# Values in token pairs, one fixed load order and constants on VectorE in a kernel of windowed attention and an MLP

## Chip, cores and metric

The kernel runs on one core of one Trainium2 chip. The metric is device time in microseconds (us); each number is the median of several executions. TensorE (PE in the profile) multiplies matrices, PEld is its weight load, VectorE is DVE, ScalarE is ACT, GpSimd is POOL, SyncE is SP (SPq is its queue, which issues the DMAs).

## The reference, cut to what matters

```python
# q, k, v: (4 batches, 8 heads, 768 tokens, 64); 4 sink tokens, window 128
scores = q @ k.T / 8
keep = is_sink | in_window            # token sees the 4 sinks and the last 128
a = softmax(where(keep, scores, -1e9))
x = (a @ v) as (3072 tokens, 512)
h = x @ w_in                          # 512 x 2048, "up projection"
out = (h * sigmoid(1.702 * h)) @ w_out   # 2048 x 512, "down projection"
```

All inputs and the output are fp32 in HBM; the kernel computes in fp16. It works on 12 tiles of 256 tokens (three per batch).

## The kernel before

All work is recorded as operations with estimated durations. A planner inside the kernel then picks, on each engine, the operation that can start first, and that gives the order of every engine's instruction stream. The order of each stream is then fixed, so a wrong estimate or a late load holds up everything behind it. One queue (SyncE) issues nearly all loads and all stores.

Weights come in eight chunks of 1 MB in fp32 through two staging buffers, and GpSimd casts each in two halves:

```python
def weights(j, at):
    dst = w32[j % RW]                        # RW = 2
    war = reuse("w32", j % RW)               # wait for the casts of chunk j - 2
    ...
    o_l = op("SP", 420, (2700,), lambda: nc.sync.dma_start(dst, src), war, prio=at, kind="w")
    for n in range(2):
        ...
        o = op("POOL", 1170, 1300, lambda to=to, fr=fr: nc.gpsimd.tensor_copy(out=to, in_=fr), [o_l], ...)
```

q and k are loaded with two neighbouring tokens per partition, so a contiguous piece is 2 x 64 x 4 = 512 B. v is loaded so that row p of half i holds token 2p + i, which makes 256 B pieces and four DMAs per tile; one GpSimd cast follows:

```python
for j in range(2):
    for i in range(2):
        def f(i=i, j=j):
            nc.sync.dma_start(
                dv[64 * i : 64 * i + 64, j],
                v[b, :, t0 + P * j : t0 + P * j + P].rearrange("h (p i) d -> i p h d", i=2)[i],
            )
...
def f():
    nc.gpsimd.tensor_copy(out=w16[:, :, :, 0:D], in_=dv)
```

Constants (ones columns, zeroed sink keys `ks16`, zeroed sink values `vs16`) are set by GpSimd; the sink values are loaded in fp32 and cast by GpSimd into `vs16`.

The softmax here doesn't subtract the row's maximum and nothing guards it: scores larger than these inputs give would overflow.

## Time and profile before

| | before |
|---|---|
| time, median | 260.92 us |
| profiled span | 258.1 us |
| time between the start of tile 7's and tile 10's up projection | 55.2 us (18.4 per tile) |
| last chunk of w_out landed | 98.9 us |
| first matmul of tile 7's up projection | 159.6 us |

(A landing is the end of a DMA in the trace. The start of a tile's projection is found by counting: the up projection has 768 matmul records, 64 per tile, in order.)

The page's slices, from kernel before. Each digit is the busy share of one fortieth of the span in tenths; PEclk is the TensorE clock that was granted, GB/s what the DMA moved.

```profile
PE   8987897799959969999999999999999999999991
PEclk9997999999998997999999999999999999999999
DMA  7999999999999999893310110111011011011132
GB/s 208 227 230 343 211 222 216 346 230 207 240 355 226 209 316 254 199 221 84 83 43 0 43 41 3 41 43 24 19 42 44 1 43 41 3 41 43 41 70 51
```

The DMA is full for the first 18 slices (6.45 us each, so to about 116 us). TensorE has gaps in the first 16 (103 us) and is then full to the end. Where the GB/s are over 340, weights are moving; where they are 207 to 230, q, k and v are.

The same in four stretches of the kernel before: busy us (number of instructions) of each engine, then granted clock, DMA share and GB/s.

```profile
core 0: us, PE busy (x) PEld busy (x) DVE busy (x) ACT busy (x) POOL busy (x), PEclk, DMA share, GB/s
0.00:30.00 30.00, 25.20 (x336) 20.20 (x337) 20.73 (x49) 12.21 (x25) 21.30 (x51) 0.94 1.05 241
30.00:60.00 30.00, 26.28 (x324) 20.88 (x322) 25.79 (x63) 19.46 (x40) 19.03 (x29) 1.00 1.17 258
60.00:104.00 44.00, 38.60 (x415) 27.12 (x412) 30.27 (x70) 24.39 (x51) 20.82 (x31) 0.92 1.08 254
104.00:240.00 136.00, 136.00 (x1210) 87.68 (x1209) 72.31 (x160) 69.26 (x130) 12.73 (x24) 1.00 0.23 52
```

From 104 us TensorE is busy 136.00 of 136. What can be gained lies before.

Who uses the staging buffers of the weights, kernel before: durations min/median/max in ns, first and last start, then who waited for these instructions (us, times).

```profile
L303 POOL CAST w_in<-w x8: 1036/1042/1504, 21.3 to 52.5; 128x1024 f16<-128x1024 f32 x8
L303 POOL CAST w_out<-w x8: 1041/1044/1047, 75.7 to 100.0; 128x1024 f16<-128x1024 f32 x8
...
who waited for it (us, times):
  PE bank L580: 5.1, 2
...
  PEld L552: 3.1, 4
  PE bank L552: 2.2, 2
```

DMA packets by size, kernel before. Of those under 512 B, 24,576 are v's (one of 256 B for each of 3072 tokens and 8 heads).

```profile
DMA packets 59074, 34.22 MB, mean 133 GB/s; under 512 B 27048, under 2 KB 52008, under 8 KB 59048
```

### The profile page before, as it was taken

The numbers are of one execution on the slowest core, as the hardware profiler recorded it, in microseconds if no ns is written. First come the engines' busy times: TensorE is split into PE (matmuls) and PEld (weight loads), VectorE is DVE, ScalarE is ACT, GpSimd is POOL, SyncE is SP. The second block draws the span as 40 slices with busy tenths as digits, with TensorE's granted clock in tenths as the row PEclk, the third lists the DMA queues.
The fourth block names the chain that finished last, engine by engine and source line by source line (L and its number), as shares of the span: only waits on it lengthen the run. The fifth ranks groups of instructions, "written<-read, shape, count | busy, mean of one in ns | idle before, by whom it ended". The sixth has DMA issues, their size and how long they took to land.

```text
span 258.1 us, 5883 instructions
## 1 busy us (share of the span) xinstructions
PE 238.5 (92%) x2344; PEld 162.4 (63%) x2344; DVE 151.8 (59%) x345; ACT 129.0 (50%) x250; POOL 73.9 (29%) x133
## 2 busy tenths in 40 slices
PE   8987897799959969999999999999999999999991
PEld 8755675687835854444566667666666666666640
DVE  4866899689952983100167766776766666553310
ACT  0726495468742762211265575555557557533411
POOL 8666657661545248200010130131300000000000
PEclk9997999999998997999999999999999999999999
DMA  7999999999999999893310110111011011011132
GB/s 208 227 230 343 211 222 216 346 230 207 240 355 226 209 316 254 199 221 84 83 43 0 43 41 3 41 43 24 19 42 44 1 43 41 3 41 43 41 70 51
DMA packets 59074, 34.22 MB, mean 133 GB/s; under 512 B 27048, under 2 KB 52008, under 8 KB 59048
## 3 DMA queue, kind: packets, MB, share of 16 engines
q1 hardware_dynamic: 57816, 33.10, 56.3%
q10 hardware_dynamic: 1232, 0.75, 1.0%
q8 instruction: 18, 0.29, 0.5%
q14 instruction: 8, 0.07, 0.2%
HBM read 27.56 MB, written 6.29 MB: 131 GB/s over the span
## 4 chain that ended last, share of the span: by engine, by line
PE 66%; DMA 18%; SPq 6%; POOL 4%; issue 2%; DVE 1%; ACT 0%; ACTq 0%; POOLq 0%
PE bank L580 31%; PE bank L552 23%; DMA w<-in_moe_w_in_dram 6%; DMA qk<-in_q_dram 5%; SPq L349 5%; PE bank L498 3%; PE bank L444 3%; DMA w<-in_moe_w_out_dram 3%; PE bank L407 3%; POOL qk L371 2%; DMA v<-in_v_dram 2%; DMA mask<-cmask 2%; PE bank L523 1%; SPq L339 1%; DMA qk<-in_k_dram 1%
## 5 line engine op out<-in xcount | busy, mean ns | idle before, releaser
L580 PE MATMUL bank<-w_out,gT 128*128 128x512 f16 x384 | 101.8, 387 | 5.1 <-POOL w_out L303 5.1
L552 PE MATMUL bank<-xT,w_in 128*128 128x256 f16 x768 | 102.4, 274 | 2.3 <-POOL w_in L303 2.2
L552 PEld LDWEIGHTS <-w_in 128*128 128x128 f16 x768 | 72.2, 98 | 21.3 <-POOL w_in L303 3.1
L566 DVE SCALAR_TENSOR_TENSOR gT<-th,bank 128x512 f16<-128x512 f16 x96 | 65.1, 679 | 28.9 <-ACT th L564 28.8
L564 ACT ACTIVATE th<-bank 128x512 f16<-128x512 f32 x96 | 57.5, 599 | 46.9 <-PE bank L552 44.7
L459 ACT ACTIVATE at<-bank 128x512 f16<-128x512 f32 (+1 forms) x96 | 48.6, 565 | 22.2 <-PE bank L444 22.2
L580 PEld LDWEIGHTS <-gT 128*128 128x128 f16 x384 | 35.3, 99 | 28.5 <-issue 8.4
L371 POOL CAST qk<-qk 128x512 f16<-128x512 f32 x44 | 27.7, 658 | 55.3 <-PE bank L407 50.2
L465 DVE TENSOR_TENSOR at<-at,mask 128x1024 f16<-128x1024 f16 (+1 forms) x48 | 35.4, 738 | 8.5 <-ACT at L459 8.0
L531 DVE COPY xT<-bank 128x256 f16<-128x256 f16 x48 | 13.7, 285 | 29.4 <-ACT th L564 21.7
L600 ACT ACTIVATE osb<-bank 128x512 f32<-128x512 f32 (+1 forms) x25 | 14.3, 579 | 28.9 <-PE bank L580 28.9
L415 DVE COPY qkT<-bank 128x512 f16<-128x512 f16 x48 | 20.0, 419 | 9.8 <-PE bank L407 9.3
L498 PE MATMUL bank<-v,at 128*128 128x65 f16 x352 | 21.7, 194 | 0.9 <-DVE at L465 0.9
L481 ACT ACTIVATE ats<-bank 128x256 f16<-128x256 f32 x32 | 12.4, 386 | 19.4 <-PE bank L474 14.2
L498 PEld LDWEIGHTS <-at 128*128 128x128 f16 x352 | 17.9, 98 | 5.6 <-DVE at L465 1.6
L515 DVE TENSOR_TENSOR xn<-bank,rcp 128x256 f16<-128x256 f32 x48 | 20.2, 422 | 1.1
L383 POOL CAST v<-v 128x1024 f16<-128x1024 f32 x12 | 13.0, 1080 | 27.0 <-DMA v<-in_v_dram 18.0
L407 PE MATMUL bank<-ident,qk 128*128 128x128 f16 x192 | 18.3, 220 | 0.9 <-POOL qk L371 0.7
L444 PE MATMUL bank<-qkT 64*128 64x256 f16 x192 | 16.2, 246 | 0.8 <-DVE qkT L415 0.4
L513 DVE RECIPROCAL rcp<-bank 128x4 f32<-128x4 f32 x48 | 8.5, 176 | 12.7 <-PE bank L498 9.3
L407 PEld LDWEIGHTS <-qk 128*128 128x128 f16 x192 | 12.2, 97 | 5.8 <-issue 3.5
L498 PE MATMUL bank<-vs,ats 128*128 128x65 f16 x128 | 15.4, 195 | 0.2
(24 smaller groups left out, 121.0 us busy)
## 6 DMA issues: line engine op xcount, KB each, us to landing
v<-in_v_dram SPq DMA_DIRECT2D x48, 128.0 KB, 5.7
out_dram<-osb SPq DMA_DIRECT2D x46, 128.0 KB, 2.4
qk<-in_q_dram SPq DMA_DIRECT2D x11, 512.0 KB, 6.2
qk<-in_k_dram SPq DMA_DIRECT2D x11, 512.0 KB, 8.0
w<-in_moe_w_in_dram SPq DMA_DIRECT2D x4, 1024.0 KB, 7.9
w<-in_moe_w_out_dram SPq DMA_DIRECT2D x4, 1024.0 KB, 7.8
qk<-in_k_dram ACTq DMA_DIRECT2D x4, 128.0 KB, 3.0
qk<-in_q_dram SPq DMA_DIRECT2D x4, 128.0 KB, 3.2
```

The lines of the kernel that those rows point to most:

```text
L371: nc.gpsimd.tensor_copy(out=c16[:, :, e, h].rearrange("s i h d -> s h i d"), in_=dst[:, e, h])
L407: nc.tensor.transpose(ps[:, e, :, i, :], c16[:, i, e, 2 * p : 2 * p + 2].rearrange("s h d -> s (h d)"), ident)
L415: o_cp = op("DVE", 331, 430, lambda: nc.vector.tensor_copy(out=T, in_=f16(o_tp).rearrange("d (e j s) -> d e j s", e=2, j=2)), [o_tp] + war ...
L444: nc.tensor.matmul(f32(o_s, i)[:, c : c + w], src[d, 1, j], T[d, 0].rearrange("d j s -> d (j s)")[:, q0 : q0 + w], start=True, stop=True,)
L459: nc.scalar.activation(out=A[:, i, 0:W], in_=f32(o_s, i)[:, 0:W], func=AF.Exp, scale=scale)
L465: nc.vector.tensor_tensor(out=A[:, :, 0:W], in0=A[:, :, 0:W], in1=mask[:, c0 : c0 + W].unsqueeze(1).to_broadcast((P, 2, W)), op=ALU.mult,)
L498: nc.tensor.matmul(ps[:, j, i], a_, v_, start=(n == 0), stop=(n == len(mms) - 1))
L515: o_n = op("DVE", 300, 425, lambda: nc.vector.tensor_tensor(out=X, in0=avp()[:, :, :, 0:D], in1=rc.to_broadcast((P, 2, 2, D)), op=ALU.mult ...
L552: nc.tensor.matmul(f32(holder[0])[:, bass.ts(e, TB)], w_in16[:, c, bass.ts(Fi, P)], X[:, c], start=(c == 0), stop=(c == NP - 1),)
L564: o_t = op("ACT", 477, 600, lambda first=first: nc.scalar.activation(out=th[first.places[0]], in_=f32(first), func=AF.Tanh, scale=0.851), ...
L566: o_g[k, s] = op("DVE", 565, 690, lambda first=first, s=s: nc.vector.scalar_tensor_tensor(out=g[:, 2 * s : 2 * s + 2].rearrange("p a t -> ...
L580: nc.tensor.matmul(f32(holder[0]), g[:, Fi, bass.ts(j, P)], w_out16[:, Fi], start=(Fi == 0), stop=(Fi == NF - 1),)
```

## The change

Its intent: full-size packets for v, weights early, and a shorter start. v is loaded like q and k; the rows then sit at the wrong partitions, so four casts of 64 partitions put them right. All big loads are chained in one order of priority: tiles 0 and 1, all of w_in, tile 2, all of w_out, then tiles 3 to 11. Weights get a third staging buffer. Constants go to VectorE, and the sink values are cast by a DMA issued by GpSimd. Attention outputs and their transposes may hold two PSUM banks (of the eight in TensorE's result memory) each instead of one.

```diff
-    RS, RQ, RV, RKT, RA, RX, RG, RTH, RO, RW = 3, 2, 4, 9, 6, 3, 5, 3, 3, 2
+    RS, RQ, RV, RKT, RA, RX, RG, RTH, RO, RW = 3, 2, 4, 9, 6, 3, 5, 3, 3, 3
-    plan = Plan(8, {"s": 4, "k": 1, "t": 2, "a": 1, "x": 1, "h": RTH, "o": 2})
+    plan = Plan(8, {"s": 4, "k": 1, "t": 2, "a": 2, "x": 2, "h": RTH, "o": 2})
+    o_ks0 = op("DVE", 600, 700, lambda: nc.vector.memset(ks16, 0.0), ...)
+    def vs_const():
+        nc.vector.memset(vs16, 0.0)
...
+            nc.gpsimd.dma_start(
+                vs16[32 * i : 32 * i + 4, :, :, i, 0:D], v[:, i::2, 0:n_sink, :].rearrange("b h t d -> t b h d")
+            )
...
-        for j in range(2):
-            for i in range(2):
-                ...                                  # four loads of 64 partitions
+        o_lv = op("SP", 450, (1790,), lambda: nc.sync.dma_start(
+            dv, v[b, :, t0 : t0 + TB].rearrange("h (p i) d -> p h i d", i=2)), war, prio=prio + 0.6, kind="load")
...
-            nc.gpsimd.tensor_copy(out=w16[:, :, :, 0:D], in_=dv)
+        for j in range(2):
+            for i in range(2):
+                    nc.gpsimd.tensor_copy(
+                        out=w16[64 * i : 64 * i + 64, j, :, 0:D], in_=dv[64 * j : 64 * j + 64, :, i]
+                    )
...
+    loads.sort(key=lambda o: (o.prio, o.seq))
+    for a_, b_ in zip(loads, loads[1:]):
+        b_.behind = a_                               # the planner starts b_ only after a_
```

(Cut: the planner's test of `behind`, its new estimates for DMA latency, and the order of the small loads: the identity goes from SyncE's queue to ScalarE's, the mask after it.)

More of the change, by code (lines that the diff above doesn't have):

```diff
@@ L44 @@
         "eng", "dur", "lat", "fn", "deps", "prio", "acq", "rel", "start", "end", "left", "users",
-        "seq", "banks", "places", "kind",
+        "seq", "banks", "places", "kind", "behind",
     )
@@ L53, in __init__ @@
         self.users = []
-        self.banks = None
+        self.banks = self.behind = None
 HOP = {
@@ L97, in could @@
         def could(o, t):
+            if o.behind and o.behind.start is None:
+                return None
             s = max([t] + [after(d, o) for d in o.deps])
@@ L140, in run @@
             if isinstance(o.lat, tuple):
-                begin = max(s + 1500, dma_free)
+                begin = max(s + 2000, dma_free)
                 dma_free = begin + o.lat[0]
-                o.end = dma_free + 500
+                o.end = dma_free + 300
             else:
@@ L208 @@
     w32 = ring("w32", RW, (P, 4, 512), FP32)
-    vs32 = pool.tile([P, B, NP, D], FP32, name="vs32")
     vs16 = pool.tile([P, B, NP, 2, E], FP16, name="vs16")
-    ks16 = ring("ks16", B * NP, (P, P), FP16)
+    ks16 = pool.tile([P, B * NP, P], FP16, name="ks16")
     qk32 = ring("qk32", RS, (P, 2, H, 2, D), FP32)
-    v32 = ring("v32", RS, (P, 2, H, D), FP32)
+    v32 = ring("v32", RS, (P, H, 2, D), FP32)
     qk16 = ring("qk16", RQ, (P, 2, 2, H, D), FP16)
@@ L248 @@
     o_zero = op("DVE", 100, 200, lambda: nc.vector.memset(zero, 0.0), prio=NEVER, kind="const")
-    o_ident = op("SP", 420, (140,), lambda: nc.sync.dma_start(ident, ident_d.ap()), prio=NEVER + 2.3, kind="load")
-    o_mask = op("ACT", 420, (400,), lambda: nc.scalar.dma_start(mask, mask_d.ap()), prio=NEVER + 3, kind="load")
-    o_vs0 = op("POOL", 1800, 2000, lambda: nc.gpsimd.memset(vs16, 0.0), prio=NEVER + 120, kind="const")
-    def vs_ones():
+    o_ident = op("ACT", 420, (140,), lambda: nc.scalar.dma_start(ident, ident_d.ap()), prio=NEVER + 2.6, kind="load")
@@ L254, in vs_ones, with ones @@
+    o_mask = op("ACT", 420, (400,), lambda: nc.scalar.dma_start(mask, mask_d.ap()), prio=NEVER + 4, kind="load")
+    def ones():
+        for t in v16:
+            nc.vector.memset(t[:, :, :, D : D + 1], 1.0)
+    o_ones = op("DVE", 250, 350, ones, prio=NEVER + 1, kind="const")
+    o_ks0 = op("DVE", 600, 700, lambda: nc.vector.memset(ks16, 0.0), prio=NEVER + 2, kind="const")
+    def vs_const():
+        nc.vector.memset(vs16, 0.0)
         for i in range(2):
-            nc.gpsimd.memset(vs16[32 * i : 32 * i + 4, :, :, i, D : D + 1], 1.0)
@@ L257 @@
-    o_vs1 = op("POOL", 300, 400, vs_ones, [o_vs0], prio=NEVER + 121, kind="const")
+            nc.vector.memset(vs16[32 * i : 32 * i + 4, :, :, i, D : D + 1], 1.0)
+    o_vs0 = op("DVE", 700, 800, vs_const, prio=NEVER + 3, kind="const")
     def vs_load():
         for i in range(2):
-            nc.sync.dma_start(
-                vs32[32 * i : 32 * i + 4], v[:, i::2, 0:n_sink, :].rearrange("b h t d -> t b h d")
-            )
-    o_vsl = op("SP", 900, (300,), vs_load, prio=NEVER + 10, kind="load")
@@ L267, in vs_cast @@
-    def vs_cast():
-        for i in range(2):
-            r = slice(32 * i, 32 * i + 4)
-            nc.gpsimd.tensor_copy(out=vs16[r, :, :, i, 0:D], in_=vs32[r])
-    o_vsc = op("POOL", 2400, 2500, vs_cast, [o_vsl, o_vs1], prio=NEVER+122, kind="vs")
-    o_ks0 = []
-    for u in range(B * NP):
-        o_ks0.append(
-            op("POOL", 150, 250, lambda u=u: nc.gpsimd.memset(ks16[u], 0.0), prio=NEVER + 12 + 40 * (u // NP), kind="const")
-        )
-    o_one = []
-    for i in range(RV):
-        o_one.append(
-            op("POOL", 120, 220, lambda i=i: nc.gpsimd.memset(v16[i][:, :, :, D : D + 1], 1.0),
-               prio=NEVER + 10 + i, kind="const")
-        )
+            nc.gpsimd.dma_start(
+                vs16[32 * i : 32 * i + 4, :, :, i, 0:D], v[:, i::2, 0:n_sink, :].rearrange("b h t d -> t b h d")
+            )
@@ L287 @@
+    o_vs = op("POOL", 2000, (300,), vs_load, [o_vs0], prio=NEVER + 10, kind="load")
     o_win, o_wout = {}, {}
+    loads = []
     def weights(j, at):
@@ L295, in weights @@
             src = moe_w_out[bass.ts(j - 4, 512), :].rearrange("(c p) f -> p c f", p=P)
-        o_l = op("SP", 420, (2700,), lambda: nc.sync.dma_start(dst, src), war, prio=at, kind="w")
+        o_l = op("SP", 450, (3000,), lambda: nc.sync.dma_start(dst, src), war, prio=at, kind="w")
+        loads.append(o_l)
         for n in range(2):
@@ L334, in f @@
                         )
-                    lq[p, e] = op(eng, 420, (432,), f, war, prio=NEVER + 2.5 + p / 8, kind="load")
+                    lq[p, e] = op(eng, 500, (450,), f, war, prio=NEVER + 2.5 + p / 8, kind="load")
         else:
@@ L341, in f @@
                     )
-                o = op("SP", 420, (1730,), f, war, prio=prio + e, kind="load")
+                o = op("SP", 450, (1790,), f, war, prio=prio + e / 2, kind="load")
+                loads.append(o)
                 for p in range(NP):
                     lq[p, e] = o
-        lv = []
-        for j in range(2):
-            for i in range(2):
-                def f(i=i, j=j):
-                    nc.sync.dma_start(
-                        dv[64 * i : 64 * i + 64, j],
-                        v[b, :, t0 + P * j : t0 + P * j + P].rearrange("h (p i) d -> i p h d", i=2)[i],
-                    )
-                lv.append(op("SP", 420, (560,), f, war, prio=prio + 2 + i, kind="load"))
+        o_lv = op("SP", 450, (1790,), lambda: nc.sync.dma_start(
+            dv, v[b, :, t0 : t0 + TB].rearrange("h (p i) d -> p h i d", i=2)), war, prio=prio + 0.6, kind="load")
+        loads.append(o_lv)
         c16 = qk16[k % RQ]
@@ L380, in load, with f @@
         war = reuse("v16", k % RV)
-        def f():
-            nc.gpsimd.tensor_copy(out=w16[:, :, :, 0:D], in_=dv)
-        o_cv[k] = op("POOL", 1200, 1300, f, lv + war + [o_one[k % RV]],
-                     prio=(nominal(k - 1, -4) if k else NEVER + 5), kind="cv")
-        uses("s32", sl, o_cv[k])
+        o_cv[k] = []
+        for j in range(2):
+            for i in range(2):
+                def f(j=j, i=i):
+                    nc.gpsimd.tensor_copy(
+                        out=w16[64 * i : 64 * i + 64, j, :, 0:D], in_=dv[64 * j : 64 * j + 64, :, i]
+                    )
+                o = op("POOL", 560, 660, f, [o_lv] + war + [o_ones],
+                       prio=(nominal(k - 1, -4) if k else NEVER + 5), kind="cv")
+                o_cv[k].append(o)
+                uses("s32", sl, o)
     k_ap = k
@@ L423, in ks @@
                     nc.gpsimd.tensor_copy(
-                        out=ks16[NP * b + p][d, 32 * i : 32 * i + 4].rearrange("d (a i) -> d i a", i=2),
+                        out=ks16[d, NP * b + p, 32 * i : 32 * i + 4].rearrange("d (a i) -> d i a", i=2),
                         in_=T[d, 1, 0].rearrange("d (i a) -> d i a", i=2)[:, :, 0:2],
                     )
-            o_ks[b, p] = op("POOL", 260, 400, ks, [o_cp, o_ks0[NP * b + p]], prio=base - 4 * h8, kind="ks")
+            o_ks[b, p] = op("POOL", 260, 400, ks, [o_cp, o_ks0], prio=base - 4 * h8, kind="ks")
             uses("qkT", u % RKT, o_ks[b, p])
@@ L474, in sk @@
                 nc.tensor.matmul(
-                    f32(o_k)[:, 0:TB], ks16[NP * b + p], T[:, 0].rearrange("d j s -> d (j s)"),
+                    f32(o_k)[:, 0:TB], ks16[:, NP * b + p], T[:, 0].rearrange("d j s -> d (j s)"),
                     start=True, stop=True,
@@ L500, in attention @@
         dur = 12 * 31 if r else 6 * 31
-        deps = [o_m, o_cv[k]] + ([o_se, o_cv[k - 1], o_vsc] if r else [])
+        deps = [o_m, *o_cv[k]] + ([o_se, *o_cv[k - 1], o_vs] if r else [])
         o_a = op("PE", dur, dur + 166, av, deps, prio=base - 1.5 * h8, acq=("a", 1), kind="av")
```

## The prediction

> What bounds the kernel now. The median is 260.94 us, the profiled span 258.1. The slices show two stages. Up to about 115 us the DMA is full (9 tenths in nearly every slice) and TensorE has gaps; from 104 us TensorE runs back to back (20.00 us busy in each 20 us window) until its last matmul at 252.4, a tail of 5.7. In steady state a tile of 256 tokens costs 18.4 us (up projection of tile 7 starts at 159.6, of tile 10 at 214.8), all TensorE. The chain of waits agrees: DMA 18%, queue issue 6%, nearly all before 100 us. So the loss is TensorE's starved time before 104 us.
>
> What changes.
> - v packets. 24,832 packets of 256 B (27.9 ns mean, 43.3 us over 16 engines) beside 24,576 of 512 B for q and k (32.9 ns). v now gets half as many of 512 B, as q, about 25 us: 18 us less. The records add up to 1.1 times the elapsed time there, so about 1.3 us per tile, 16 in all. The Trainium skill, "DMA: Bandwidth & Descriptors", Specifications, gives 512 B as the minimum for line rate; this trace agrees: 9.2 B/ns against 15.6 per engine. v takes 12 issues instead of 48.
> - Load order. w_in goes straight after tile 1, w_out after tile 2, with three staging buffers. Before, the last w_out landed at 98.9 us, and the first down projection waited for it while tiles 3 to 8 were loaded. This is the larger part: the dense stretch can start after three tiles.
> - GpSimd casts v in four pieces of 64 partitions, about 0.6 us each instead of one of 1.08: plus 1.2 us per tile. It loses memsets (5 us) and the 2.4 us sink cast.
> - Constants on VectorE fall where it idles until q arrives (0.9 to 3.1 us): nothing. The casting DMA is needed only at 18 us: nothing.
>
> Estimate. Rates from landings: 1 MB of weights 2.9 us, 512 KB of q, k or v 1.95. Tile 0's q and k are in at 8.2 as now, v at 9.4, tile 1 at 15.3, w_in at 26.9, tile 2 at 32.8, w_out at 44.4; two casts of 1.05 make it usable at 46.5. The new instruction order puts half of the first down projection and two pieces of the up projection after that (about 5 us), so the steady pattern starts with tile 2's up projection at 52. Five tiles at 18.4 lead to tile 7's at 144, where it was at 159.6; from there the TensorE order is the same, 92.8 us to the last matmul and 5.7 to the end. Span 242.5, time about 245. The gain, 16 us, is TensorE idle time before 52.
>
> Expected: 244.5 us, range 238 to 251; faster by over 2% 0.94, within 2% 0.05, slower 0.01.
>
> Shown right by: the last w_out landing near 44 instead of 99 us; no 256 B packets but the sinks'; TensorE's dense stretch beginning near 50; the tile period unchanged at 18.4; loads done near 100 instead of 115.
>
> What would make it wrong: GpSimd (about 32 us of casts before 46) falling behind the weights, since VectorE's mask multiply and GpSimd slow each other (that multiply took 0.55 to 1.10 us here); output stores queued behind blocked loads on the single queue; a lower TensorE clock in the denser start (0.83 in three windows before); or the w_in reload waiting for its buffer.

## More of the kernel before

The casts of w_out are spread from 75.7 to 100.0 us, and the down projection (L580) waited 5.1 us for them, in two waits of 2.8 and 2.3 us. The up projection (L552) waited for w_in.

## The result and the profile after

| | before | after |
|---|---|---|
| time, median | 260.92 us | 246.81 us |
| ratio to before, 95% interval | | 0.9466 [0.9429, 0.9504] |
| profiled span | 258.1 us | 244.4 us |
| last chunk of w_out landed | 98.9 us | 46.0 us |
| start of tile 7's up projection | 159.6 us | 146.4 us |
| tile 7 to tile 10 | 55.2 us | 55.1 us |

A ratio is the mean time of one kernel's fast runs over that of the other's of the same rounds, so it is not quite the ratio of the medians quoted. In the kernel after, source lines have moved: the up projection is L544 (was L552), the down projection L572 (L580), weight casts L294 (L303), q and k casts L357 (L371), v casts L373 (L383).

The page's slices, kernel after:

```profile
PE   8968899999999999999999999999999999999991
PEclk9999999999999999999999999999999999999998
DMA  6999999999999914902901101101101101101132
GB/s 175 263 340 329 334 355 347 305 288 302 247 293 303 290 58 112 236 3 58 285 4 43 46 3 43 42 4 46 43 3 46 43 3 43 44 2 46 43 73 55
```

The stretches of the kernel after (columns as before):

```profile
0.00:30.00 30.00, 24.16 (x333) 19.26 (x334) 23.40 (x61) 12.22 (x25) 20.50 (x34) 1.00 0.99 288
30.00:60.00 30.00, 29.82 (x308) 21.14 (x306) 20.38 (x47) 17.15 (x35) 23.73 (x37) 1.00 1.09 318
60.00:104.00 44.00, 44.00 (x457) 29.93 (x454) 30.17 (x68) 26.29 (x52) 21.49 (x35) 1.00 0.85 223
```

Weight casts and who waited for them, kernel after:

```profile
L294 POOL CAST w_in<-w x8: 1037/1164/1499, 19.6 to 29.4; 128x1024 f16<-128x1024 f32 x8
L294 POOL CAST w_out<-w x8: 1035/1165/1498, 36.8 to 47.0; 128x1024 f16<-128x1024 f32 x8
...
who waited for it (us, times):
  POOL w_out L294: 2.3, 3
  POOL w_in L294: 1.3, 3
```

And its packets:

```profile
DMA packets 46618, 34.20 MB, mean 140 GB/s; under 512 B 2304, under 2 KB 39552, under 8 KB 46592
```

What to see: TensorE is full after the first 5 slices (30 us) instead of 16. It was busy 29.82 of 30 us between 30 and 60, and 44.00 of 44 between 60 and 104. Nobody on TensorE waits for a weight cast any more; the only one listed is GpSimd itself, waiting for its next chunk. v's small packets are gone. The first 30 us did not improve: 24.16 us busy against 25.20, and those figures include filler matmuls that are meant to keep the clock up.

Then a surprise: TensorE's total busy time fell from 238.5 to 233.1 us, though the matmuls are the same but for the fillers (136 and 131). The clock explains most of that. Three windows of the kernel before, each 3.41 us long, which the trace records at half clock:

```profile
21.61:25.02 3.41, 2.65 (x23) 2.15 (x24) 1.54 (x3) 1.87 (x4) 2.53 (x3) 0.50 1.12 324
76.22:79.63 3.41, 2.79 (x7) 1.01 (x7) 0.00 (x0) 0.00 (x0) 2.82 (x4) 0.50 1.17 310
96.70:100.11 3.41, 2.99 (x12) 1.11 (x12) 0.29 (x1) 0.44 (x2) 2.48 (x4) 0.50 1.16 318
```

And the 3.41 us just before each of them:

```profile
18.20:21.61 3.41, 2.26 (x34) 1.26 (x31) 3.12 (x6) 3.25 (x9) 1.38 (x2) 1.00 1.06 384
72.81:76.22 3.41, 1.22 (x12) 0.95 (x10) 2.03 (x4) 1.41 (x4) 1.69 (x2) 1.00 1.05 385
93.29:96.70 3.41, 1.53 (x21) 1.09 (x20) 2.88 (x7) 1.88 (x4) 1.45 (x2) 1.00 1.03 378
```

TensorE was busy for only 2.26, 1.22 and 1.53 us of these, and was then run at half clock for one window. In the second and third it waited for w_out (2.8 and 2.3 us, the waits above); in the first mainly for VectorE's mask multiplies and copies. In the three slow windows it was busy 8.43 us at half clock, so about 4.2 us of its work would have fitted into half the time: an estimate of 4.2 us lost, of the 5.4 us difference in busy time. The profiled run of the kernel after has no such window before its last matmul. The Trainium skill, "TensorE: Matmul & The Clock Gate", Part 1, describes this gate as half rate after an idle window of about 3.4 us; the length agrees with the 3.41 us here, but the windows that led to it were a third to two thirds busy.

### The profile page after: what moved, and what is told of

Same layout as the page of the kernel before. It is cut to its first block, busy times and chain, and to the rows that moved or that the text cites. A ratio compares the mean times of both kernels' runs of the same rounds, so it can differ in the third digit from the quotient of the medians.

```text
span 244.4 us, 5826 instructions
## 1 busy us (share of the span) xinstructions
PE 233.1 (95%) x2339; PEld 160.0 (65%) x2339; DVE 154.7 (63%) x353; ACT 129.4 (53%) x250; POOL 87.3 (36%) x146
## 2 busy tenths in 40 slices
DMA packets 46618, 34.20 MB, mean 140 GB/s; under 512 B 2304, under 2 KB 39552, under 8 KB 46592
## 4 chain that ended last, share of the span: by engine, by line
PE 84%; DVE 6%; DMA 4%; ACT 2%; issue 0%; ACTq 0%; DVEq 0%
PE bank L572 34%; PE bank L544 33%; PE bank L490 5%; PE bank L436 5%; PE bank L399 5%; DVE at L457 3%; DMA mask<-cmask 3%; PE bank L515 2%; DVE xn L507 1%; PE bank L466 1%; ACT at L451 1%; DMA ident<-cident 1%; DVE gT L558 1%; ACT th L556 0%; ACT ats L473 0%; DVE xT L523 0%
## 5 line engine op out<-in xcount | busy, mean ns | idle before, releaser
L572 PE MATMUL bank<-w_out,gT 128*128 128x512 f16 x384 | 107.0, 379 | 0.0
L544 PE MATMUL bank<-xT,w_in 128*128 128x256 f16 x768 | 103.0, 273 | 0.7 <-DVE xT L523 0.6
L544 PEld LDWEIGHTS <-w_in 128*128 128x128 f16 x768 | 72.7, 98 | 22.9 <-issue 2.4
L572 PEld LDWEIGHTS <-gT 128*128 128x128 f16 x384 | 33.4, 98 | 9.9 <-issue 0.2
L357 POOL CAST qk<-qk 128x512 f16<-128x512 f32 x44 | 26.9, 643 | 34.1 <-PE bank L399 31.6
L373 POOL CAST v<-v 64x512 f16<-64x512 f32 x48 | 31.2, 649 | 14.7 <-PE bank L490 11.8
L399 PE MATMUL bank<-ident,qk 128*128 128x128 f16 x192 | 18.4, 221 | 0.4 <-DVE qk L348 0.2
L415 POOL COPY ks<-qkT 64x4 f16<-64x4 f16 x32 | 8.9, 277 | 26.2 <-DVE qkT L407 22.6
L515 PEld LDWEIGHTS <-xn 128*128 128x128 f16 x96 | 8.7, 98 | 11.6 <-DVE xn L507 2.8
```

Of the source, the lines that this page charges most:

```text
L357: nc.gpsimd.tensor_copy(out=c16[:, :, e, h].rearrange("s i h d -> s h i d"), in_=dst[:, e, h])
L373: nc.gpsimd.tensor_copy(out=w16[64 * i : 64 * i + 64, j, :, 0:D], in_=dv[64 * j : 64 * j + 64, :, i])
L399: nc.tensor.transpose(ps[:, e, :, i, :], c16[:, i, e, 2 * p : 2 * p + 2].rearrange("s h d -> s (h d)"), ident)
L544: nc.tensor.matmul(f32(holder[0])[:, bass.ts(e, TB)], w_in16[:, c, bass.ts(Fi, P)], X[:, c], start=(c == 0), stop=(c == NP - 1),)
L572: nc.tensor.matmul(f32(holder[0]), g[:, Fi, bass.ts(j, P)], w_out16[:, Fi], start=(Fi == 0), stop=(Fi == NF - 1),)
```

## The experiments

Twelve kernels ran. Names A to E are the theories, as the expectations introduce them. Ratios are to the kernel before in the same rounds; its median was 262.08, 260.98 and 261.12 us in the three groups.

| run | median us | ratio | 95% interval |
|---|---|---|---|
| e1_v256 | 248.65 | 0.9497 | [0.9464, 0.9531] |
| e2_pairs_only | 251.50 | 0.9595 | [0.9563, 0.9627] |
| e9_order_only | 250.01 | 0.9545 | [0.9520, 0.9571] |
| e3_free_order | 249.48 | 0.9539 | [0.9487, 0.9592] |
| after_again (control) | 246.92 | 0.9460 | [0.9426, 0.9494] |
| e5_rw4 | 247.96 | 0.9501 | [0.9467, 0.9535] |
| e6_mask | 246.04 | 0.9436 | [0.9397, 0.9475] |
| e13_vs_pool | 246.87 | 0.9463 | [0.9430, 0.9496] |
| e7_consts | 249.43 | 0.9559 | [0.9521, 0.9596] |
| e8_banks1 | 248.18 | 0.9521 | [0.9483, 0.9560] |
| e15_v0_act | 244.86 | 0.9396 | [0.9353, 0.9439] |
| e16_v0_act_mask | 244.87 | 0.9395 | [0.9353, 0.9436] |

All were correct. The planner makes a new TensorE order for most of these edits (in e1_v256, e5_rw4, e13_vs_pool and the control it is that of the changed kernel, fillers aside), so a run compares two plans, not one load alone. Not tested alone: the third staging buffer, the planner's new DMA estimates, and the identity's move to ScalarE's queue.

### Packets or order?

**The changed kernel with v in 256 B packets.** The instruction order of TensorE is the same.

```diff
-    o_lv = op("SP", 450, (1790,), lambda: nc.sync.dma_start(dv, v[...].rearrange("h (p i) d -> p h i d", i=2)), ...)
+    def f_lv():                       # the four loads of the kernel before, in one planned operation
+        for j in range(2):
+            for i in range(2):
+                nc.sync.dma_start(dv[64 * i : 64 * i + 64, j], v[...].rearrange("h (p i) d -> i p h d", i=2)[i])
-    in_=dv[64 * j : 64 * j + 64, :, i]
+    in_=dv[64 * i : 64 * i + 64, j]
```

> The changed kernel with v loaded as before, in four issues of 256 B packets per tile; casts stay in four pieces (no rows moved), and the instruction order on every engine stays that of the changed kernel. Theory A (the load order is the larger part, and TensorE has some slack): the last w_out lands about 4 us later (three v tiles at 1.35 us), near 50 us, and the time is 248 to 251 us. Theory B (the packets are the larger part): 254 us or more.

It took 248.65 us: 1.8 us over the changed kernel by the medians, but 0.8 us by the ratios (this group's kernel before was slower too), with overlapping intervals. The last w_out landed at 49.5 us instead of 46.0, but tile 2's up projection started at 53.8 instead of 52.6. So 3.5 us of later loading cost 1.2 us: with weights early, the packets hardly matter. Theory B falls for this kernel; the time and the landing are those of Theory A. One down projection did wait here, 1.1 us, for a cast of w_out; in the changed kernel none did.

**The kernel before with token pairs alone.**

```diff
-    four loads "h (p i) d -> i p h d" and one cast of 128 partitions
+    one load "h (p i) d -> p h i d" and four casts of 64 partitions (as in the change)
```

> The kernel before with v loaded in token pairs (512 B packets, one issue per tile) and cast in four pieces, nothing else; two staging buffers for weights and the load order are left to its planner. Theory A (order is the larger part): the last w_out still lands after 85 us and the time stays at 254 us or more. Theory B (packets): 250 us or less. Theory C (the two overlap, since either lets TensorE fill the same idle time): this and e9_order_only each give more than 8 of the 14 us.

251.50 us: 10.6 us of gain by this part alone, far more than A allowed. The last w_out landed at 84.3 us instead of 98.9, in the old order. Who waited for weight casts in this run:

```profile
who waited for it (us, times):
  PEld L549: 1.1, 1
  PE bank L549: 0.8, 1
```

The down projection's waits of 5.1 us are gone (only the up projection, here L549, waits), and with them both half-clock windows near 76 and 97 us; this trace has 6.8 us at half clock, all near 16 to 22 us.

**The kernel before with the fixed order and the third buffer alone.**

```diff
+    "behind", and loads.sort(...); b_.behind = a_     (as in the change)
-    RW = 2
+    RW = 3
```

> The kernel before with the one fixed load order and three staging buffers for weights, nothing else: v still comes in 256 B packets, constants and casts stay on GpSimd. Theory A: 248 to 251 us, as e1_v256. Theory B: 255 us or more. Theory C: about 250 us, and e2_pairs_only close to it.

250.01 us: 12.1 us of gain, with v still in 256 B packets. Together with the run above this is Theory C: one part alone gives 4.05%, the other 4.55%, both with the rest of the change 5.34%, not 8.6%. Both fill the same idle time of TensorE. Once it is full, more loading speed buys little. The run e7_consts below supports this: it has fixed order, third buffer, token pairs and second banks together, with the constants on GpSimd as here, and is no faster (0.9559) than this run without token pairs and second banks (0.9545).

**The changed kernel without the chain that fixes the order.**

```diff
-    for a_, b_ in zip(loads, loads[1:]):
-        b_.behind = a_
```

> The changed kernel without the chain that fixes the load order: its planner then puts the fourth w_in and all of w_out after more tiles (a staging buffer that is not free lets other loads pass). Theory A: slower than the changed kernel by 3 us or more (250 or over), with the last w_out landing after 50 us. Theory B: within 1.5 us of the changed kernel's 246.8.

249.48 us. The planner put the last two chunks of w_out after tile 7, and the last landed at 73.7 us. The interval just overlaps the changed kernel's, so a cost of 2.7 us by the medians, 1.9 by the ratios, is likely, not certain, and lies between what Theories A and B allowed (its profiled run, the slowest of its four, also has a half-clock window from 10.71 to 14.12 us). It is small beside the 28 us by which w_out is later, because TensorE then has up projections and attention of other tiles to do.

### What sets the place of the dense stretch?

The dense stretch is the part in which TensorE has no gaps. The prediction took the last landing of w_out (Theory D). The view of the weight casts in the profile after says otherwise: no matmul waited for w_out. Theory E is that TensorE is dense from 29 us on and that the start-up of the first two tiles decides.

**The control.** 

> The changed kernel itself, as the control for the three runs beside it: ratio to the kernel before 0.945 to 0.950 by every theory.

246.92 us, 0.9460: the first result repeats. Its trace, too, has no half-clock window before the last matmul.

**A fourth staging buffer.** `RW = 4` instead of 3, the same TensorE order.

> The changed kernel with four staging buffers for weights instead of three; the TensorE order stays the same. The fourth w_in and the fourth w_out no longer wait for a cast, so the last w_out lands 1.5 to 2.5 us earlier. Theory D (the prediction's: TensorE's dense stretch is set by the last w_out's landing): 1.5 to 2.5 us faster than the control. Theory E (TensorE has been dense since about 29 us, and its position is set by the start-up of the first two tiles' attention): within 0.5 us of the control.

247.96 us, not faster. But the premise failed: the last w_out landed at 45.4 us, against 45.2 in the control. Probably the wait for a buffer had been hidden behind other transfers. So this run does not tell D from E; it shows only that the fourth buffer brings nothing.

**The mask early.** 

```diff
-    o_mask = op("ACT", 420, (400,), lambda: nc.scalar.dma_start(mask, ...), prio=NEVER + 4, ...)
+    o_mask = op("SP", 420, (400,), lambda: nc.sync.dma_start(mask, ...), prio=NEVER + 2.95, ...)
```

> The changed kernel with the mask's load issued on the SyncE queue before tile 0's v and tile 1, so that it lands near 8 us instead of 11.7. VectorE waited 1.5 us for it before the first mask multiply. Theory E: 0.7 to 1.5 us faster than the control. Theory D: within 0.5 us.

246.04 us; 0.9 us under the control by the medians, but the intervals overlap widely, so nothing is shown by the time. The trace shows why little came of it. VectorE in the changed kernel's first profile, in the control's, then in this run (start us, length us, what, and in brackets the idle time before it and what ended it):

```profile
11.78 3.30 DVE L457 TENSOR_TENSOR at<-at,mask 128x768 f16<-128x768 f16 x4 [1.54 <-DMA mask<-cmask]
15.01 0.17 DVE L505 RECIPROCAL rcp<-bank 128x4 f32<-128x4 f32 x1
```

```profile
10.65 2.37 DVE L457 TENSOR_TENSOR at<-at,mask 128x768 f16<-128x768 f16 x4
15.15 0.18 DVE L505 RECIPROCAL rcp<-bank 128x4 f32<-128x4 f32 x1 [2.13 <-PE bank L490]
```

```profile
9.34 0.56 DVE L457 TENSOR_TENSOR at<-at,mask 128x768 f16<-128x768 f16 x1 [0.33 <-ACT at L451]
...
12.42 0.56 DVE L457 TENSOR_TENSOR at<-at,mask 128x768 f16<-128x768 f16 x1 [0.87 <-ACT at L451]
15.11 0.18 DVE L505 RECIPROCAL rcp<-bank 128x4 f32<-128x4 f32 x1 [2.13 <-PE bank L490]
```

Against the first profile the multiplies start 2.4 us earlier and the last ends at 13.0 instead of 15.1, but the next instruction starts at 15.11, not earlier than 15.01: it waits 2.13 us for the attention output, and that needs v, which landed at 10.8 us and which GpSimd was still casting. The wait moved. In the control, the same kernel as the first profile, the mask had landed in time (10.0 us) without the edit, and VectorE waited the same 2.13 us; so the mask was not the limit. This run's profile also has one half-clock window (22.93 to 26.34 us) that the control lacks. A multiply took 0.55 to 0.56 us here; in the first profile, beside GpSimd's v casts, the four took 0.65, 0.96, 0.96 and 0.96. The Trainium skill, "SBUF — State Buffer", Who interferes with whom, says that a VectorE instruction with two SBUF inputs contends with a GpSimd instruction that reads SBUF; these numbers agree.

**Sink constants on GpSimd.** 

```diff
-    nc.vector.memset(vs16, 0.0)  and two small ones
+    nc.gpsimd.memset(vs16, 0.0)  and two small ones, op("POOL", 2300, 2400, ...)
```

> The changed kernel with the sink values' constants (one memset of 128x2080, 1.79 us on VectorE, and two small ones) set on GpSimd, which is idle there, instead of VectorE. The first q cast on VectorE can start near 3.5 us instead of 4.83. If those constants delay the start-up (against the prediction's 'nothing'): 0.5 to 1.2 us faster than the control. If the last k piece's landing (9.1 us) and the mask's set the end of tile 0's attention anyway: within 0.4 us.

246.87 us, as the control. VectorE's first q cast started at 3.64 instead of 4.83 us, and nothing came of it. The prediction had these constants end by 3.1 us; they ended at 4.8, and it did not matter.

**Constants and sinks all on GpSimd, as before.**

```diff
-    memsets on VectorE; sinks by a casting DMA into vs16
+    memsets on GpSimd; sinks by a plain DMA into vs32, then nc.gpsimd.tensor_copy(out=vs16[...], in_=vs32[...])
```

> The changed kernel with its constants set on GpSimd and the sinks loaded in fp32 and cast by GpSimd, both as in the kernel before; everything else as changed. Prediction ('nothing'): ratio to the kernel before 0.943 to 0.950, as the control's 0.946. Rival (GpSimd's queue is the start-up's critical engine between 10 and 20 us, so that the 2.4 us sink cast there delays tile 1's casts): 0.952 or more.

249.43 us; the interval lies clear of the control's. Here are GpSimd's instructions in the changed kernel, then in this run:

```profile
10.77 3.02 POOL L373 CAST v<-v 64x512 f16<-64x512 f32 x4
13.85 2.82 POOL L357 CAST qk<-qk 128x512 f16<-128x512 f32 x4
16.86 2.59 POOL L373 CAST v<-v 64x512 f16<-64x512 f32 x4 [0.19 <-DMA v<-in_v_dram]
```

```profile
11.13 3.05 POOL L387 CAST v<-v 64x512 f16<-64x512 f32 x4
14.24 2.15 POOL L273 CAST vs<-vs 4x1024 f16<-4x1024 f32 x2
16.45 1.17 POOL L371 CAST qk<-qk 128x512 f16<-128x512 f32 x2
17.56 2.58 POOL L387 CAST v<-v 64x512 f16<-64x512 f32 x4
20.20 1.63 POOL L371 CAST qk<-qk 128x512 f16<-128x512 f32 x2
```

The sink cast (2.15 us) stands between tile 0's v and tile 1's q and k, and the planner's order then puts tile 1's v between the two halves of q and k. Tile 1's q and k are ready at 21.8 us instead of 16.7. The run also has one half-clock window, from 21.78 to 25.19 us, that the control lacks. How much of the 2.5 us is the delay and how much the clock was not separated.

**One bank each for attention outputs and transposes.** `"a": 1, "x": 1` instead of 2.

> The changed kernel with one bank each for attention outputs and transposes, as before, instead of two. If the second bank only matters in the first two tiles: slower than the control by 0.3 to 1.5 us (ratio 0.947 to 0.952) with the period from tile 7 to tile 10 unchanged; if it shortens the dense stretch, that period (55.1 us for three tiles) grows.

248.18 us, 1.3 us over the control by the medians; the intervals overlap a little. Tile 0's last transpose ended at 21.0 us instead of 18.2, tile 7 to tile 10 took 55.2 us as ever, and one half-clock window (17.02 to 20.43 us) appears. So the second bank helps, if at all, only in the start-up.

**Tile 0's v cast on ScalarE.** 

```diff
-    nc.gpsimd.tensor_copy(out=w16[...], in_=dv[...])            # op("POOL", 560, 660, ...)
+    (nc.gpsimd.tensor_copy if k else nc.scalar.copy)(out=w16[...], in_=dv[...])   # op("POOL" if k else "ACT", ...)
```

> The changed kernel with the four casts of tile 0's v on ScalarE, which is idle from 11.6 to 18.5 us, instead of GpSimd, so that GpSimd casts tile 1's q and k as they land (14.8 us) and does not slow VectorE's mask multiplies. Theory E (the start-up chain v cast, tile 1's casts, attention sets where TensorE's dense stretch lies): tile 1's transposes start near 16 us instead of 17.2 and the time is 0.7 to 1.5 us under the control, ratio 0.940 to 0.944. Theory D (the last w_out): ratio 0.946.

244.86 us, 2.1 us under the control by the medians and the fastest so far; the intervals overlap slightly, and the two ran on different chips. GpSimd in this run:

```profile
13.21 2.80 POOL L357 CAST qk<-qk 128x512 f16<-128x512 f32 x4 [2.18 <-DMA qk<-in_q_dram]
17.02 3.08 POOL L373 CAST v<-v 64x512 f16<-64x512 f32 x4 [1.01 <-DMA v<-in_v_dram]
```

It now waits for q and k to land, and casts them by 16.0 us. Tile 1's transposes started at 15.9 us (control 17.3) and tile 2's up projection at 51.6 (control 52.7), although the last w_out landed later than in the control (45.4 against 45.2 us). That speaks for E and against D.

**The same with the mask early.** Both edits above.

> As e15_v0_act, with the mask issued early as in e6_mask. Theory E: as fast as e15_v0_act or up to 1 us faster, ratio 0.937 to 0.943; the wait of VectorE for the attention output of tile 0 (2.1 us in e6_mask) is gone. Theory D: ratio 0.946.

244.87 us, no different from the run before. Its profiled execution had a span of 242.8 us and tile 2's up projection at 50.5, with the last w_out at 46.2 us: the dense stretch came 2.2 us earlier than in the control with w_out 1.1 us later. That is not what D allows. By the medians these two kernels beat both the kernel before and the changed one; their intervals still overlap the control's by about 0.001.

## Why the prediction was right, and where it was not

- **The time.** 244.5 us with 238 to 251 was predicted, 246.81 measured. The start of tile 2's up projection was given as 52 and came at 52.6. The five tiles from there to tile 7 were put at 92 us and took 93.8: the mis-sized term is the period of the first tile, 19.6 us (52.6 to 72.2) instead of 18.4, since all of tile 3's attention and the beginning of tile 4's fall into it. From tile 7 on, 98.0 us to the end of the span against 98.5. The steady period itself, 55.1 us for three tiles, held.
- **Where the gain lies.** "The gain, 16 us, is TensorE idle time before 52" was wrong. Up to 52 us TensorE was busy 43.48 us in the kernel before and 45.99 in the kernel after, only 2.5 us more; from 52 to 104 us it was 46.60 and 51.98, 5.4 us more. Most of the rest of the 13.7 us of span is work that the kernel before did at half clock.
- **Weights early.** Last w_out near 44 us predicted, 46.0 measured, and TensorE full from there: right. But "two casts of 1.05 make it usable at 46.5 [...] so the steady pattern starts with tile 2's up projection at 52" was the wrong reason for the right number. TensorE was already full from 30 us (29.82 of 30), no matmul waited for w_out, and moving the start-up moved the dense stretch while w_out stayed (e15, e16). The two limits lay close together.
- **Packets and order.** The saving of packet time was right: v's small packets are gone (27,048 under 512 B became 2,304), and e2 shows that w_out lands 14.6 us earlier by them alone. "This is the larger part", said of the order, is not certain: 12.1 us against 10.6 when each is done alone, with intervals that overlap a little. The prediction missed that the two are not to be added.
- **Constants and the casting DMA: "nothing".** Half right. Setting the largest of them on VectorE costs nothing (e13). Taking them off GpSimd is worth about 2.5 us (e7; how much of it by the clock was not separated), because GpSimd's queue is in the start-up chain. The prediction listed these as lost work of GpSimd and gave them no value.
- **The second banks** got no value; about 1.3 us (e8), likely.
- **The clock.** The prediction named a lower clock as a danger of the denser start. It was the other way: the starved kernel had three half-clock windows, the denser one none, an estimated 4.2 us of TensorE's busy time. What a full clock alone would have gained was not tested: a later wait for w_out would have taken part of it back.
- **Loads done near 100 us instead of 115**: wrong, the last load landed at 122.3. The slices show the DMA no longer full after 85 us; the late loads wait for buffers, with no harm.
- **Dangers that did not come true**: GpSimd kept pace with the weights (last w_out cast over at 48.1, 2.1 us after its landing), and no store held up the dense stretch.

## What to carry to other kernels

When one engine is the limit in the steady state, count what a change gives it before the point where it is full; several changes that each feed it earlier share one pot and do not add up. Look for the limit of the start-up on the engine that does the odd jobs (here GpSimd's casts), not only in the transfers, and give one of its jobs to an engine that idles at that moment. Waits on TensorE can cost more than themselves: the two for w_out in the kernel before, 2.8 and 2.3 us, each came with a half-clock window in which another 1.4 and 1.5 us were lost (estimates: half of the 2.79 and 2.99 us busy in it).

## What the Trainium skill lacked or had wrong

- "TensorE: Matmul & The Clock Gate", Part 1, speaks of an idle window of about 3.4 us before half rate. Here windows with TensorE busy 2.26, 1.22 and 1.53 of 3.41 us were each followed by exactly one window of 3.41 us at half clock. In e6_mask the window from 19.52 to 22.93 us (2.29 us busy) was followed by half clock, but the one from 12.69 to 16.10 us, three windows earlier (1.89 us busy), was not, so the busy time alone does not decide. What a window needs to keep the clock is what a kernel writer needs, and the page lacks it.
- "DMA: Bandwidth & Descriptors", Specifications, gives 512 B as the minimum for line rate. By the packet records of the kernel after, 512 B took 31.8 ns on average (16.1 B/ns for one engine) and 2,048 B took 107.7 ns (19.0 B/ns); 256 B in the kernel before took 27.9 ns (9.2 B/ns). So 512 B is much better than 256 B and still below the rate of the 2,048 B packets (those of the weights and the output).
- No page that I found gives the cost of GpSimd casts that move rows to other partitions: 64 partitions x 512 elements took 0.608 us (median of 48), 128 x 1024 took 1.043 us (median of 12, kernel before). Without moving rows the 64 x 512 cast took 0.610 us (e1_v256), and 128 x 512 took 0.614 us (q and k, kernel after). So here the time follows the elements per partition: half the partitions save nothing, and moving the rows costs nothing.
